# Reloads by full rows, strided weight-gradient stores and paced V loads in a memory-bound attention-block backward kernel

## Chip, cores, metric

One core of one Trainium2 chip. The metric is the device time of one launch in microseconds (us), and shorter is better. Executions of one kernel mostly agree within 0.3% to 0.4%. So differences of a few microseconds are read from repeated rounds on one chip, where each kernel runs in turn with the kernel before. A ratio is the mean time of one kernel's runs over that of the other's runs in the same rounds, so it is not quite the ratio of the medians that are quoted.

## The reference

Forward and backward of a decode block: an adaptive layer norm, cached attention over 32 heads and 8192 keys for a batch of 2, a gated feed-forward, and the gradients of everything, the caches included. Cut to what matters:

```python
x:(2,1,512)  k_cache, v_cache:(2,32,8192,128)  wq:(512,4096)  wo:(4096,512)
w1,w3:(512,1376)  w2:(1376,512)  w_mod:(512,3072)          # all bfloat16
mod = silu(c) @ w_mod ;  h = LN(x)*(1+ca)+sa
q = h @ wq ; p = softmax(q·K/sqrt(128)) ; o = p·V ;  x = x + ga * (o @ wo)
x = x + gb * (silu(h2@w1) * (h2@w3)) @ w2
return out, d_x, d_k_cache, d_v_cache, d_wq, d_wo, d_w1, d_w3, d_w2, d_c, d_w_mod
```

K and V are 134 MB each. V is read nearly twice (once forward, once for its transposed product with the output's gradient), K once, and dK and dV are written once, 268 MB. That is almost all of the 713.56 MB that move.

## The kernel before

Work is laid out in slots. One slot is one group of eight 128x128 transposes on TensorE, and a head is eight slots. An "A" job does the forward of one head and a "C" job its backward. Between them, once per batch element, stands a "chain": output projection, feed-forward, their gradients. `t1` is the slot at which the second chain is done; behind it come some 31 C heads, and with them 196 small tasks that make the weight gradients. All big data lives in 21 buffers of 1 MB ("halves": half of one head's K or V, or of its dK or dV). SyncE's queue issues the loads in program order, and each waits until its buffer is free.

```python
def load_v(key, i, hf):
    t = htile()                                     # one of the 21 halves
    qd.dma_start(t[:], src_of(A_v_cache, i)[:, hf*HK:(hf+1)*HK, :])   # qd = nc.sync
    free["half"] -= 1
    V[(key, hf)] = t

def pump():                                         # called whenever a half is given back
    while loads and free["half"] - keep[0] >= 1:    # loads: sorted by the slot that needs them
        loads.pop(0)[2]()

def outer(store, dst, n, which, w2, q):             # dV or dK of head n, a quarter at a time
    ...
    nc.vector.tensor_tensor(pair(t[:, o:o+QK, :]), ..., ALU.mult)     # VectorE, 1.2 us
    if o + QK == HK:
        sq_.dma_start(src_of(dst, n)[:, hf*HK:(hf+1)*HK, :], t[:])    # sq_ = nc.gpsimd
        ...                                         # the half is given back six slots later

# weight gradients: a matmul of two rows, ScalarE's copy to a staging tile, a store from GpSimd's queue
for h0 in range(0, H, 4):
    def dst(st, h0=h0):
        sq_.dma_start(out_5.rearrange("(h p) d -> p h d", p=P)[:, h0:h0+4, :],
                      st[:, 0:4*D].rearrange("p (h d) -> p h d", h=4))
    wgrad(dst, [("O", (h0+k)*P, P, "d_attn", 0, D, k*D) for k in range(4)], 4)

def again(w, n):                                    # wq, w_mod a second time, in pieces of 1024 columns
    for pc in range(n-1, -1, -1):
        loads.insert(0, (0, 0, lambda pc=pc: load_piece(wqr, w, pc)))
    pump()

def chain_done():                                   # at slot t1
    wn.clear(); wo_v.clear(); release(4 + H // WH)
    for k in range(2):
        rowst[k] = hflat(); free["half"] -= 1
    pump()

per = max(1, -(-nt // max(1, room)))                # here 1: one task per slot from t1 on
for k, f in enumerate(tasks):
    at(t1 + 1 + k // per, PL_TASK, f)
```

## Time and profile before

| | |
|---|---|
| median of 6 runs (range) | 1751.83 us (1750.34 to 1755.11) |
| span of the profiled run | 1749.5 us |
| moved | 713.56 MB, 408 GB/s |
| busiest compute engine | TensorE, 79% |

The first lines are of the page of the kernel before: TensorE's granted clock, the mean busy share of the 16 DMA engines and what they moved, in 40 equal slices of the span, then the DMA queues (packets, MB, share of the engines' time). Queue 1 is the loads, queue 0 the stores, queues 8 and 14 fetch instructions.

```profile
PEclk9999999988978888888897888676755565765786
DMA  9999999999999999999999999999999999999997
GB/s 381 417 418 418 418 417 390 418 376 416 420 423 409 410 415 422 412 415 420 415 411 408 411 413 394 370 413 412 425 422 418 407 413 404 420 425 417 410 390 305
...
q1 hardware_dynamic: 73376, 425.81, 60.1%
q0 software_dynamic: 41216, 284.22, 39.1%
q8 instruction: 188, 3.08, 0.7%
```

The DMA engines are full in 39 of 40 slices: this is a kernel bound by its transfers. The next table is the view by windows. Its last three columns are TensorE's granted clock, the mean DMA share and GB/s.

```profile
core 0: us, PE busy (x) PEld busy (x) DVE busy (x) ACT busy (x) POOL busy (x), PEclk, DMA share, GB/s
1150.00:1200.00 50.00, 42.10 (x590) 40.28 (x588) 35.48 (x82) 30.36 (x38) 5.87 (x11) 0.59 1.01 413
1200.00:1225.00 25.00, 21.02 (x346) 19.94 (x343) 19.16 (x42) 14.03 (x17) 3.20 (x6) 0.63 1.01 420
1225.00:1300.00 75.00, 54.51 (x674) 41.39 (x673) 45.30 (x47) 47.55 (x78) 11.35 (x20) 0.64 1.01 424
1300.00:1650.00 350.00, 259.03 (x3194) 198.20 (x3192) 219.34 (x241) 216.20 (x329) 63.15 (x115) 0.60 1.01 416
1650.00:1735.00 85.00, 46.83 (x848) 44.15 (x848) 76.48 (x80) 41.26 (x57) 15.97 (x30) 0.74 0.96 391
1735.00:1749.00 14.00, 0.00 (x0) 0.00 (x0) 0.00 (x0) 0.00 (x0) 0.00 (x0) 0.50 0.29 120
```

In these windows everything is at 413 to 424 GB/s and a share of 1.01 until 1650 us. (Packets overlap a little: at the end of the trace packets of 309 ns follow each other every 306 ns on one engine, so a full engine shows just over 1.) Then it falls to 391 and 0.96, with VectorE busy 76.48 of 85 us. The view of the V loads' line gives, after the colon, the shortest, median and longest issue in ns, then the first and last start:

```profile
L177 SPq DMA_DIRECT2D half<-in_A_v_cache_dram x252: 327/328/6146, 22.4 to 1648.6; - x126
```

So behind 1648.6 us only stores are issued, and nearly all that moves in the last 85 us is stores. The view of the load queue's own waits for 1190 to 1225 us:

```profile
SPq L177 <- DMA out_dram<-half: 20.6, 4, 8.9
SPq L177 <- PE tp L366: 6.9, 2, 5.1
```

Here the loads wait for their buffers (for a store that has to land, or for the transposes that still read the buffer), at most 8.9 us at a time.

### The profile page before, as it was taken

What the parts mean: (1) busy time and instruction counts of PE and PEld (TensorE: products, weight loads), DVE (VectorE), ACT (ScalarE), POOL (GpSimd) and SP (SyncE); (2) the same over time, 40 slices, a digit from 0 to 9 for tenths busy, and PEclk for the clock granted to TensorE, in tenths of its full rate; (3) what the DMA queues carried; (4) which work ended last, traced back from release to release, by engine and by line L of the source; (5) the groups of instructions that cost most, each with busy time, mean ns of one, the idle gap of its engine ahead of it and who ended that gap; (6) DMA issues with size and microseconds to landing.
All of it is one profiled execution on the core that took longest, in us unless ns stands there. A gap on an engine that the chain in (4) does not pass through costs nothing. (4 is left out here: it accounts for less than half of the span.)

```text
span 1749.5 us, 54974 instructions
## 1 busy us (share of the span) xinstructions
PE 1374.4 (79%) x24112; PEld 1227.8 (70%) x24112; DVE 1170.0 (67%) x1677; ACT 980.9 (56%) x1404; POOL 393.6 (22%) x685
## 2 busy tenths in 40 slices
PE   6999999989977767777777778788686877767662
PEld 5999998979866767676676668778554655655562
DVE  2666666857776676667667668777566675756596
ACT  4666666646544445455454555565655675765562
POOL 0334333312221222122122222111112121112121
PEclk9999999988978888888897888676755565765786
DMA  9999999999999999999999999999999999999997
GB/s 381 417 418 418 418 417 390 418 376 416 420 423 409 410 415 422 412 415 420 415 411 408 411 413 394 370 413 412 425 422 418 407 413 404 420 425 417 410 390 305
DMA packets 114845, 713.56 MB, mean 408 GB/s; under 512 B 11392, under 2 KB 20300, under 8 KB 33196
## 3 DMA queue, kind: packets, MB, share of 16 engines
q1 hardware_dynamic: 73376, 425.81, 60.1%
q0 software_dynamic: 41216, 284.22, 39.1%
q8 instruction: 188, 3.08, 0.7%
q14 instruction: 53, 0.43, 0.1%
q10 hardware_dynamic: 12, 0.01, 0.0%
HBM read 425.79 MB, written 284.20 MB: 406 GB/s over the span
## 5 line engine op out<-in xcount | busy, mean ns | idle before, releaser
L371 ACT COPY kt<-tp 128x1024 bf16<-128x1024 bf16 x768 | 774.9, 1015 | 532.8 <-PE tp L366 524.4
L366 PE MATMUL tp<-identb,half 128*128 128x128 bf16 x8192 | 767.7, 249 | 2.8 <-DMA half<-in_A_k_cache_dram 1.4
L366 PEld LDWEIGHTS <-half 128*128 128x128 bf16 x8192 | 596.6, 112 | 116.7 <-issue 111.7
L1093 POOL DMA_DIRECT2D out_dram<-half x256 | 136.7, 534 | 966.8 <-DVE half L1088 810.1
L427 PE MATMUL m_ps<-ek,half 128*128 128x129 bf16 x4096 | 327.0, 222 | 0.2
L369 DVE COPY kt<-tp 128x1024 bf16<-128x1024 bf16 x256 | 175.8, 687 | 188.7 <-PE tp L366 183.6
L1065 PE MATMUL s_ps<-DO_bf,kt 128*128 128x1 bf16 x4096 | 191.3, 168 | 102.2 <-DVE kt L369 70.1
L1065 PEld LDWEIGHTS <-kt 128*128 128x128 bf16 x4096 | 186.4, 107 | 117.7 <-DVE kt L369 78.4
L386 PE MATMUL s_ps<-qT_bf,kt 128*128 128x1 bf16 x4096 | 177.8, 164 | 99.3 <-DVE kt L369 98.4
L427 PEld LDWEIGHTS <-half 128*128 128x128 bf16 x4096 | 247.7, 98 | 0.4 <-issue 0.2
L386 PEld LDWEIGHTS <-kt 128*128 128x128 bf16 x4096 | 159.6, 98 | 104.2 <-DVE kt L369 102.5
L1213 ACT CAST stg<-m_ps 128x512 bf16<-128x512 f32 (+2 forms) x123 | 72.0, 591 | 111.7 <-DMA out_dram<-stg 86.3
L1212 PE MATMUL m_ps<-half 2*128 2x512 bf16 (+2 forms) x123 | 72.3, 588 | 27.0 <-ACT stg L1213 25.2
L449 PE MATMUL k_ps<-half,pz 128*32 128x512 bf16 x1024 | 68.7, 389 | 21.0 <-POOL pz L435 21.0
L449 PEld LDWEIGHTS <-pz 128*32 128x32 bf16 x1024 | 21.8, 97 | 41.8 <-POOL pz L435 23.2
L1313 ACT COPY kt<-tp 128x1024 bf16<-128x1024 bf16 x28 | 28.6, 1048 | 6.7 <-PE tp L1306 6.6
L398 DVE TENSOR_REDUCE nm<-s_ps 128x1 f32<-128x128 f32 x64 | 18.4, 287 | 20.4 <-PE s_ps L395 20.4
L395 PE MATMUL s_ps<-nident,rm 128*128 128x128 bf16 x64 | 15.2, 238 | 20.6 <-DVE rm L390 20.6
L1190 ACT CAST half<-m_ps 2x512 bf16<-2x512 f32 (+1 forms) x36 | 19.9, 564 | 16.5 <-DMA out_dram<-half 7.8
L712 PE MATMUL tp<-identb,half 128*128 128x128 bf16 x256 | 28.0, 277 | 0.0
L1306 PE MATMUL tp<-identb,half 128*128 128x128 bf16 x224 | 20.1, 242 | 9.0 <-DMA half<-in_A_wq_dram 4.7
L712 PEld LDWEIGHTS <-half 128*128 128x128 bf16 x256 | 23.8, 135 | 0.0
(878 smaller groups left out, 1784.2 us busy)
## 6 DMA issues: line engine op xcount, KB each, us to landing
out_dram<-half POOLq DMA_DIRECT2D x256, 1024.0 KB, 12.4
half<-in_A_v_cache_dram SPq DMA_DIRECT2D x252, 1024.0 KB, 12.9
half<-in_A_k_cache_dram SPq DMA_DIRECT2D x128, 1024.0 KB, 19.8
out_dram<-stg POOLq DMA_DIRECT2D x22, 512.0 KB, 17.0
half<-in_A_wq_dram SPq DMA_DIRECT2D x8, 1024.0 KB, 14.9
half<-in_w_mod_dram SPq DMA_DIRECT2D x6, 1024.0 KB, 16.0
half<-in_B_w_dram SPq DMA_DIRECT2D x6, 1024.0 KB, 15.2
half<-in_A_wo_dram SPq DMA_DIRECT2D x4, 1024.0 KB, 20.5
```

Source lines behind the costliest of these rows:

```text
L366: nc.tensor.transpose(tp[:, j, :], block(j), identb[:])
L369: nc.vector.tensor_copy(kt[:], tp[:])
L371: nc.scalar.copy(kt[:], tp[:])
L386: nc.tensor.matmul(S_ps[i][:, cc:cc + 1], kt[:, j, :], qT_bf[:, h, b:b + 1], start=True, stop=True)
L427: nc.tensor.matmul(m[:, 0:P + 1], vb_(i, kk), t[:, kk % QK, 0:P + 1], start=(kk == 0), stop=(kk == KK - 1), skip_group_check=True)
L449: nc.tensor.matmul(kp["ps"][NR * j:NR * (j + 1), :], pz[:, o:o + NR], K[(i, kk // HK)][:, kk % HK:kk % HK + QP, :], start=False, stop=(h = ...
L712: nc.tensor.transpose(tp[:, n * NC + dc, :], wo_of(h, dc), identb[:])
L1065: nc.tensor.matmul(DP[n][:, cc:cc + 1], kt[:, j, :], DO_bf[:, b, h:h + 1], start=True, stop=True)
L1093: sq_.dma_start(src_of(dst, n)[:, hf * HK:(hf + 1) * HK, :], t[:])
L1212: nc.tensor.matmul(ps[:lw, 0:rw], rsl(ln, lc, lw), rsl(rn, rc, rw), start=True, stop=True)
L1213: nc.scalar.copy(st["t"][:lw, o:o + rw], ps[:lw, 0:rw])
L1313: nc.scalar.copy(kt[:], tp[:])
```

## The change

Its intent: larger packets for the weight matrices that are read again and for dwo and dw2, gradient stores on ScalarE's queue, gradient tasks spread over the whole stretch, and, behind the second chain, V loads that come in bursts and no longer run as far ahead as the buffers allow, so that reads are left to mix with the stores at the end. The core of the diff, with cuts:

```diff
     def pump():
         while loads and free["half"] - keep[0] >= 1:
-            loads.pop(0)[2]()
+            need = loads[0][0]
+            if not pace["lot"]:
+                loads.pop(0)[2]()
+                continue
+            n = min(pace["lot"], len(loads))
+            if need > now[0] + pace["lead"]() or (free["half"] - keep[0] < n and need > now[0] + HG):
+                return
+            for k in range(min(n, free["half"] - keep[0])):
+                issued[0] = None
+                loads.pop(0)[2]()
+                if k == 0 and issued[0] is not None:
+                    tc.add_manual_dep(issued[0].ins, turned_last[0].ins.name, ...,
+                                      reason="loads keep pace with the heads")
 ...
-            nc.tensor.transpose(tp[:, j, :], block(j), identb[:])
+            turned_last[0] = nc.tensor.transpose(tp[:, j, :], block(j), identb[:])
 ...
+    def by_rows(outp, ln, rn, n):          # dwo, dw2: every fourth row per matmul, RT = 4
+        for r0 in range(0, n, RT * P):
+            ...
+                gq.dma_start(outp[r0:r0 + RT * np_].rearrange("(p r) d -> p (r d)", r=RT), st[:np_, 0:RT * D])
+            wgrad(dst, [(ln, r0 + k, np_, rn, 0, D, k * D) for k in range(RT)], RT)
 ...                                        # all gradient stores: gq = nc.scalar in place of nc.gpsimd
+            qd.dma_start(rows[kc], src[kc * P:(kc + 1) * P, :])     # wq, w_mod again, by full rows
 ...
     def chain_done():
         ...
+        pace["lot"] = 4
+        pace["lead"] = lambda: max(NG + NG // 2, 6 * NG - (now[0] - t1) // 2)
         pump()
 ...
-    per = max(1, -(-nt // max(1, room)))
+    def slot_of(k):
+        return t1 + 1 + k * room // nt
     for k, f in enumerate(tasks):
-        at(t1 + 1 + k // per, PL_TASK, f)
+        at(slot_of(k), PL_TASK, f)
+    for k, f in again:
+        want(slot_of(k) - NG, f)
```

`lot` is how many loads go out together, and `lead` how many slots ahead of its use a load may be placed: here 48 at `t1`, shrinking to 12 (`NG` is 8, the slots of a head). `add_manual_dep`: the first V load of each lot waits, on the chip, for the transposes that stand last in the program at the point where the lot is placed.

More of the change, by code (lines that the diff above doesn't have):

```diff
@@ L163 @@
     V = {}
+    issued = [None]
+    turned_last = [None]
     def src_of(ap, i):
@@ L176, in load_v @@
         t = htile()
-        qd.dma_start(t[:], src_of(A_v_cache, i)[:, hf * HK:(hf + 1) * HK, :])
+        issued[0] = qd.dma_start(t[:], src_of(A_v_cache, i)[:, hf * HK:(hf + 1) * HK, :])
         free["half"] -= 1
@@ L327, in want @@
         loads.append((need, seq[0], f))
+    pace = {"lot": 0, "lead": lambda: 0}
     def pump():
         while loads and free["half"] - keep[0] >= 1:
-            loads.pop(0)[2]()
+            need = loads[0][0]
[9 more added lines that the diff above has]
+                if k == 0 and issued[0] is not None:
+                    tc.add_manual_dep(issued[0].ins, turned_last[0].ins.name,
+                                      mybir.DependencyInfo(mybir.DependencyClass.Sync, mybir.DependencyReason.DATA),
+                                      reason="loads keep pace with the heads")
     def release(n=1):
@@ L1198, in row_of, with rsl, wgrad @@
             later(lambda c0=c0: part(c0))
-    def rsl(name, c0, w):
+    def rsl(name, c0, w, step=1):
         k, pb, o = rmap[name]
-        return rowst[k][pb:pb + B, o + c0:o + c0 + w]
-    def wgrad(dst, pieces, n):
+        return rowst[k][pb:pb + B, o + c0:o + c0 + (w - 1) * step + 1:step]
+    gq = nc.scalar
+    RT = 4
+    def wgrad(dst, pieces, step=1):
         st = {}
@@ L1211, in one @@
             ps = mtps()
-            nc.tensor.matmul(ps[:lw, 0:rw], rsl(ln, lc, lw), rsl(rn, rc, rw), start=True, stop=True)
+            nc.tensor.matmul(ps[:lw, 0:rw], rsl(ln, lc, lw, step), rsl(rn, rc, rw), start=True, stop=True)
             nc.scalar.copy(st["t"][:lw, o:o + rw], ps[:lw, 0:rw])
@@ L1226, with dst @@
     row_of("d_ffn", d_ffn_bf, NC, 96)
-    for h0 in range(0, H, 4):
-        def dst(st, h0=h0):
-            sq_.dma_start(out_5.rearrange("(h p) d -> p h d", p=P)[:, h0:h0 + 4, :],
-                          st[:, 0:4 * D].rearrange("p (h d) -> p h d", h=4))
-        wgrad(dst, [("O", (h0 + k) * P, P, "d_attn", 0, D, k * D) for k in range(4)], 4)
+    def by_rows(outp, ln, rn, n):
+        for r0 in range(0, n, RT * P):
+            np_ = min(RT * P, n - r0) // RT
+            assert (n - r0) % RT == 0
+            def dst(st, r0=r0, np_=np_):
+                gq.dma_start(outp[r0:r0 + RT * np_].rearrange("(p r) d -> p (r d)", r=RT), st[:np_, 0:RT * D])
+            wgrad(dst, [(ln, r0 + k, np_, rn, 0, D, k * D) for k in range(RT)], RT)
+    by_rows(out_5, "O", "d_attn", HD)
     for outp, nm in ((out_6, "d_gate"), (out_7, "d_up")):
@@ L1235, in dst @@
             def dst(st, kc=kc, outp=outp):
-                sq_.dma_start(outp[kc * P:(kc + 1) * P, :], st[:, 0:F])
-            wgrad(dst, [("h2", kc * P, P, nm, c0, min(512, F - c0), c0) for c0 in range(0, F, 512)], 3)
-    for f0 in range(0, FC, 4):
-        nf = min(4, FC - f0)
-        def dst(st, f0=f0, nf=nf):
-            full = [f for f in range(f0, f0 + nf) if fsz(f) == P]
-            if full:
-                sq_.dma_start(out_8[f0 * P:(f0 + len(full)) * P].rearrange("(k p) d -> p k d", p=P),
-                              st[:, 0:len(full) * D].rearrange("p (k d) -> p k d", d=D))
-            if len(full) < nf:
-                k = nf - 1
-                sq_.dma_start(out_8[(f0 + k) * P:F, :], st[:FL, k * D:(k + 1) * D])
-        wgrad(dst, [("hh", (f0 + k) * P, fsz(f0 + k), "d_ffn", 0, D, k * D) for k in range(nf)], nf)
+                gq.dma_start(outp[kc * P:(kc + 1) * P, :], st[:, 0:F])
+            wgrad(dst, [("h2", kc * P, P, nm, c0, min(512, F - c0), c0) for c0 in range(0, F, 512)])
+    by_rows(out_8, "hh", "d_ffn", F)
     x2 = col("x2")
@@ L1261, in out_row @@
         nc.scalar.copy(r[:], tp[:B, 0:NC, :].rearrange("p k d -> p (k d)"))
-        sq_.dma_start(dst, r[:])
+        gq.dma_start(dst, r[:])
     def task_x2():
@@ L1273, with turned, load, tr @@
     later(task_x2)
-    wqr = {}
-    def again(w, n):
-        for pc in range(n - 1, -1, -1):
-            loads.insert(0, (0, 0, lambda pc=pc: load_piece(wqr, w, pc)))
-        pump()
-    def before_last(n, f):
-        tasks.insert(len(tasks) - n, f)
+    again = []
+    acc = {}
+    def turned(src, n, vec, name):
+        rows = {}
+        hold = {}
+        steps = [(kc, m0) for kc in range(NC) for m0 in range(0, n, GRP)]
+        assert n % GRP == 0
+        def load(kc):
+            rows[kc] = hflat()[:, 0:n * P]
+            free["half"] -= 1
+            qd.dma_start(rows[kc], src[kc * P:(kc + 1) * P, :])
+        def tr(k):
+            kc, m0 = steps[k]
+            if k == 0:
+                acc[name] = mtps()
+            tp = tps.tile([P, GRP, P], BF16, name="tp", tag="tp")
+            for j in range(GRP):
+                nc.tensor.transpose(tp[:, j, :], rows[kc][:, (m0 + j) * P:(m0 + j + 1) * P], identb[:])
+            if m0 + GRP == n:
+                rows.pop(kc)
+                release()
+                pump()
+            kt = ktp.tile([P, GRP, P], BF16, name="kt", tag="kt")
+            nc.scalar.copy(kt[:], tp[:])
+            hold[k] = kt
+        def mm(k):
+            kc, m0 = steps[k]
+            kt = hold.pop(k)
+            a = acc[name][:, 0:NC * B].rearrange("p (k b) -> p k b", b=B)
+            for j in range(GRP):
+                nc.tensor.matmul(a[:, kc, :], kt[:, j, :], vec[:, m0 + j, :],
+                                 start=(k == 0 and j == 0), stop=(m0 + j == n - 1),
+                                 skip_group_check=True)
+        for k in range(len(steps) + 1):
+            if k < len(steps) and steps[k][1] == 0:
+                again.append((len(tasks), lambda kc=steps[k][0]: load(kc)))
+            later(lambda k=k: (tr(k) if k < len(steps) else None, mm(k - 1) if k else None))
     row_of("dq", hv(DQ_bf), H, 32)
@@ L1291, in dst @@
             def dst(st, kc=kc, half=half, w=w):
-                sq_.dma_start(out_4[kc * P:(kc + 1) * P, half * w:(half + 1) * w], st[:, 0:w])
-            wgrad(dst, [("h1", kc * P, P, "dq", half * w + c0, 512, c0) for c0 in range(0, w, 512)], 4)
-    acc = {}
-    def turned(n, vec, name):
-        hold = {}
-        def tr(m0):
-            if m0 == 0:
-                acc[name] = mtps()
-            tp = tps.tile([P, GRP, P], BF16, name="tp", tag="tp")
-            for k in range(2):
-                for kc in range(NC):
-                    nc.tensor.transpose(tp[:, k * NC + kc, :],
-                                        piece(wqr, kc, m0 + k), identb[:])
-            if (m0 + 2) * P % PW == 0:
-                wqr.pop(m0 * P // PW)
-                release()
-                pump()
-            kt = ktp.tile([P, GRP, P], BF16, name="kt", tag="kt")
-            nc.scalar.copy(kt[:], tp[:])
-            hold[m0] = kt
-        def mm(m0):
-            kt = hold.pop(m0)
-            a = acc[name][:, 0:NC * B].rearrange("p (k b) -> p k b", b=B)
-            for k in range(2):
-                for kc in range(NC):
-                    nc.tensor.matmul(a[:, kc, :], kt[:, k * NC + kc, :], vec[:, m0 + k, :],
-                                     start=(m0 == 0 and k == 0 and kc == 0), stop=(m0 + k == n - 1),
-                                     skip_group_check=True)
-        later(lambda: tr(0))
-        for m0 in range(2, n, 2):
-            later(lambda m0=m0: (tr(m0), mm(m0 - 2)))
-        later(lambda: mm(n - 2))
+                gq.dma_start(out_4[kc * P:(kc + 1) * P, half * w:(half + 1) * w], st[:, 0:w])
+            wgrad(dst, [("h1", kc * P, P, "dq", half * w + c0, 512, c0) for c0 in range(0, w, 512)])
     d_h1 = col("d_h1")
@@ L1345, in task_dx0 @@
         out_row(d_x0, out_1.rearrange("b s d -> (b s) d"))
-    before_last(12, lambda: again(wq_d, HD // PW))
-    turned(H, hv(DQ_bf), "h1")
+    turned(A_wq, H, hv(DQ_bf), "h1")
     later(task_dh1)
@@ L1357, in dst @@
             def dst(st, kc=kc, m0=m0, w=w):
-                sq_.dma_start(out_10[kc * P:(kc + 1) * P, m0:m0 + w], st[:, 0:w])
-            wgrad(dst, [("sc", kc * P, P, "d_mod", m0 + c0, 512, c0) for c0 in range(0, w, 512)], 4)
-    before_last(12, lambda: again(wm_d, MD // PW))
-    turned(MC, d_mod_bf, "c")
+                gq.dma_start(out_10[kc * P:(kc + 1) * P, m0:m0 + w], st[:, 0:w])
+            wgrad(dst, [("sc", kc * P, P, "d_mod", m0 + c0, 512, c0) for c0 in range(0, w, 512)])
+    turned(w_mod, MC, d_mod_bf, "c")
     def task_dc():
@@ L1382 @@
     room = max(sC) - NG - t1 - 2
-    per = max(1, -(-nt // max(1, room)))
+    assert room > 0
+    def slot_of(k):
+        return t1 + 1 + k * room // nt
     for k, f in enumerate(tasks):
-        at(t1 + 1 + k // per, PL_TASK, f)
+        at(slot_of(k), PL_TASK, f)
+    for k, f in again:
+        want(slot_of(k) - NG, f)
+    loads.sort(key=lambda x: x[:2])
     pump()
```

## The prediction

> **What bounds the kernel.** The DMA engines: in the page's slices their share is nine tenths or more in 39 of 40, 408 GB/s over the span; no compute engine passes 79%. 713.56 MB at the achieved rate is the time, so only a better rate or fuller engines shorten it. All of the change lies behind the second chain, whose first task (the dq matmuls, by the view of that line) runs at 1221 us. About 525 us and 217 MB are in play there, at a mean of 413 GB/s.
>
> In the table of windows, 1225 to 1650 us runs at 417 GB/s with a DMA share of 1.01, but 1650 to 1735 us at 391 GB/s and 0.96: the last V load is issued at 1648.6 us, after that there are only stores, and VectorE, which makes the dV and dK tiles, is busy 76.5 of 85 us. The loads had run ahead as far as buffers allowed, so the end has no reads to mix in and is bound by VectorE, about 10.6 us per head instead of about 15 us by DMA.
>
> **What the change does, costed with the trace's packet records.**
> 1. wq and w_mod by full rows: 3584 packets of 2 KB at 85.3 ns, against 77 ns per 2 KB of an 8 KB packet (309 ns). Saving 3584 x 8 ns / 16 engines = 1.8 us. The Trainium skill, "DMA: Bandwidth & Descriptors", section "Why small descriptors are slow (HBM only)", gives a fixed cost per packet; the trace agrees in direction.
> 2. Strided dwo and dw2: their stores are already recorded as 4 KB packets (164.5 ns; other 4 KB stores 159). At most 0.4 us.
> 3. Gradient stores from ACT's queue instead of POOL's. Same page, "Issuing engines are not separate DMA queues": all share the 16 engines, so no bandwidth. It frees about 25 us of waiting in POOL's queue, off the critical path.
> 4. Tasks spread over the whole room: gradient stores and w_mod loads move toward the end. With lead shrinking to 12 slots reads are held back, stores get buffers (VectorE waits 84 us for them in 1150 to 1650 us), and the last lot is issued about 20 slots before the last head. The write-only tail should shrink from 85 us to 25 to 40 us: 50 us x (418 - 391)/418 = 3 to 4 us.
> 5. Against it, lots alternate mixed and write-only stretches. Windows with half reads ran at 420 to 426 GB/s, with a quarter reads 405 to 415, write-only near 407 per full share. Two thirds at 421 and one third at 407 is 416, today's rate. Lots themselves: 0 to 4 us.
>
> Sum: 1.8 + 3.5 + 2 + small, about 8 us. Ceiling: all 217 MB at 424 GB/s would save 14 us; 2% (35 us) is out of reach.
>
> **Prediction:** 1743.5 us, range 1735 to 1750. Faster by over 2%: 0.03, within 2%: 0.95, slower: 0.02.
>
> **What the profile would show.** No 2 KB read packets after 1221 us; last V load 40 to 60 us nearer to the end; DMA share 1.0 until the last 30 us, VectorE no longer full for 85 us; 417 to 422 GB/s behind 1221 us; less waiting of VectorE for store buffers; gradient stores on a third queue; nothing changed before 1221 us.
>
> **What would make it wrong.** Loads held too short: PE waits for V and the DMA share dips between lots (slower). Long write-only stretches under 405 GB/s that eat the tail's gain. Or bursts of reads raise the mixed rate above 424 GB/s, unseen in this trace (below 1735 us).

## The result

| | before | changed |
|---|---|---|
| median us (range, runs) | 1752.03 (1750.04 to 1756.29, 20) | 1750.92 (1747.54 to 1754.23, 10) |
| ratio, 95% interval | | 0.9991 (0.9982 to 1.0001) |

The outputs are correct. The time is the same within 2%, as forecast, but only 1.1 us went away where 8 had been forecast, and the measured time is outside the stated range of 1735 to 1750. The same lines of the page of the changed kernel, now with a queue 10, which is ScalarE's with the gradient stores:

```profile
PEclk9999999988988978887888888665855565586585
DMA  9999999999999999999999999998999999999997
GB/s 380 417 417 417 418 417 389 417 378 416 419 423 407 413 418 422 412 409 421 412 413 407 421 407 390 379 407 336 419 422 422 415 412 419 419 418 418 425 418 295
...
q1 hardware_dynamic: 70832, 425.81, 59.7%
q0 software_dynamic: 36864, 268.45, 36.9%
q10 hardware_dynamic: 5019, 15.78, 2.3%
```

And its windows:

```profile
core 0: us, PE busy (x) PEld busy (x) DVE busy (x) ACT busy (x) POOL busy (x), PEclk, DMA share, GB/s
1150.00:1200.00 50.00, 43.45 (x564) 41.63 (x561) 34.50 (x79) 29.81 (x38) 5.87 (x11) 0.51 1.01 412
1200.00:1225.00 25.00, 22.11 (x353) 21.08 (x352) 18.71 (x41) 13.84 (x17) 3.20 (x6) 0.57 0.73 286
1225.00:1300.00 75.00, 56.36 (x768) 45.01 (x766) 56.82 (x59) 51.82 (x82) 11.19 (x21) 0.68 1.01 420
1300.00:1650.00 350.00, 262.76 (x3168) 204.62 (x3165) 222.86 (x247) 217.07 (x331) 43.15 (x81) 0.57 1.01 418
1650.00:1735.00 85.00, 44.31 (x790) 41.23 (x790) 61.09 (x64) 40.99 (x54) 12.78 (x24) 0.66 1.01 421
1735.00:1749.00 14.00, 0.00 (x0) 0.00 (x0) 0.00 (x0) 0.00 (x0) 0.00 (x0) 0.50 0.29 123
```

Two windows differ most. The end did what was predicted: 421 GB/s in place of 391 over 1650 to 1735 us, the engines full. But 1200 to 1225 us fell from 420 to 286 GB/s with a share of 0.73, which as an estimate from the two windows costs 25 x (420 - 286) / 420 = 8 us. The V loads' line and the load queue's waits for 1190 to 1225 us say what is missing there:

```profile
L179 SPq DMA_DIRECT2D half<-in_A_v_cache_dram x252: 327/328/5981, 22.5 to 1682.0; - x126
```

```profile
SPq L179 <- PE tp L383: 25.9, 1, 25.9
SPq L179 <- DMA out_dram<-half: 7.7, 1, 7.7
```

One single wait of 25.9 us for transposes. In the trace no load is issued between 1194.6 and 1221.0 us; in the kernel before eight were issued between 1200 and 1219 us. So there are two questions. Does that wait cost what the end has gained? And did the full end bring what its windows promise?

### The profile page after: what moved, and what is told of

The parts are those of the page before. It is cut to its first block, busy times and chain, and to the rows that moved or that the text cites. A ratio compares the mean times of both kernels' runs of the same rounds, so it can differ in the third digit from the quotient of the medians.

```text
span 1752.4 us, 54847 instructions
## 1 busy us (share of the span) xinstructions
PE 1382.9 (79%) x24113; PEld 1242.4 (71%) x24113; DVE 1168.4 (67%) x1677; ACT 985.1 (56%) x1405; POOL 370.5 (21%) x646
## 3 DMA queue, kind: packets, MB, share of 16 engines
q0 software_dynamic: 36864, 268.45, 36.9%
## 5 line engine op out<-in xcount | busy, mean ns | idle before, releaser
L388 ACT COPY kt<-tp 128x1024 bf16<-128x1024 bf16 x768 | 773.8, 1014 | 585.1 <-PE tp L383 573.9
L383 PE MATMUL tp<-identb,half 128*128 128x128 bf16 x8192 | 779.6, 252 | 3.9 <-DMA half<-in_A_k_cache_dram 1.5
L383 PEld LDWEIGHTS <-half 128*128 128x128 bf16 x8192 | 606.6, 113 | 91.4 <-issue 85.3
L1082 PEld LDWEIGHTS <-kt 128*128 128x128 bf16 x4096 | 191.9, 109 | 135.6 <-DVE kt L386 110.3
L444 PEld LDWEIGHTS <-half 128*128 128x128 bf16 x4096 | 246.6, 98 | 0.2
L403 PEld LDWEIGHTS <-kt 128*128 128x128 bf16 x4096 | 159.2, 98 | 107.6 <-DVE kt L386 105.7
L1315 ACT COPY kt<-tp 128x1024 bf16<-128x1024 bf16 x28 | 28.6, 1044 | 9.3 <-PE tp L1309 9.2
L729 PE MATMUL tp<-identb,half 128*128 128x128 bf16 x256 | 30.0, 292 | 0.0
L1309 PE MATMUL tp<-identb,half 128*128 128x128 bf16 x224 | 20.4, 245 | 8.5 <-DVE kt L386 8.2
L729 PEld LDWEIGHTS <-half 128*128 128x128 bf16 x256 | 25.8, 143 | 0.0
L735 ACT COPY kt<-tp 128x1024 bf16<-128x1024 bf16 x16 | 16.2, 1012 | 14.2 <-PE tp L729 13.6
## 6 DMA issues: line engine op xcount, KB each, us to landing
out_dram<-half POOLq DMA_DIRECT2D x256, 1024.0 KB, 14.6
```

Of the source, the lines that this page charges most:

```text
L383: turned_last[0] = nc.tensor.transpose(tp[:, j, :], block(j), identb[:])
L388: nc.scalar.copy(kt[:], tp[:])
L403: nc.tensor.matmul(S_ps[i][:, cc:cc + 1], kt[:, j, :], qT_bf[:, h, b:b + 1], start=True, stop=True)
L444: nc.tensor.matmul(m[:, 0:P + 1], vb_(i, kk), t[:, kk % QK, 0:P + 1], start=(kk == 0), stop=(kk == KK - 1), skip_group_check=True)
L729: nc.tensor.transpose(tp[:, n * NC + dc, :], wo_of(h, dc), identb[:])
L1082: nc.tensor.matmul(DP[n][:, cc:cc + 1], kt[:, j, :], DO_bf[:, b, h:h + 1], start=True, stop=True)
```

## The experiments

The theories, as named in the expectations: **A**, the gain at the end is real and is paid back at the one wait ahead of 1221 us. **B**, a kernel with full engines can't gain by moving reads about, and the hole is only where the moved reads are missing. Later came **C**: the end waits for one DMA engine that is behind the other fifteen, so that the mean share misleads.

### 1. The first wait taken out (e1_first_free)

```diff
-                if k == 0 and issued[0] is not None:
+                if k == 0 and issued[0] is not None and now[0] > t1:
```

A dependency is taken away here that protects no data; buffers are still waited for.

> Theory A (the tail's gain was real and was paid back at one place: the first paced load waits for the transposes of the second chain's last slot, so the load queue issues nothing from 1195 to 1221 us and the DMA share falls to 0.5 to 0.7 in 1205 to 1225 us): with only that first wait taken out the hole is gone, 1200 to 1250 us is back above 415 GB/s, the tail stays full, and the time is 1742 to 1744 us, ratio to before about 0.995. Theory B (a kernel whose engines are full cannot gain by moving reads; the hole is only where the moved reads are missing, and filling it empties the end again): 1749 to 1752 us, with the tail below 400 GB/s again or another dip.

Measured: 1745.99 us median against 1751.83 of before in the same rounds, ratio 0.9969 (0.9957 to 0.9982). 1200 to 1250 us ran at 422 GB/s. The hole is gone and the time falls by 5.8 us. That is for A, though 2 us less than A had said. The end stays full, as A said: the 85 us from 1640 to 1725 us ran at 421 GB/s and a share of 1.01. (The window of the tables above, 1650 to 1735 us, shows 384 here, because this kernel is nearly through by then: its span is 1742.4 us.)

### 2. The rows without the pace (e2_rows_only)

```diff
-        pace["lot"] = 4
-        pace["lead"] = lambda: max(NG + NG // 2, 6 * NG - (now[0] - t1) // 2)
```

> The change without the lots and the lead (by rows, strided, other queue, tasks spread). Theory A: no hole at 1200 us, packets of wq and w_mod save about 2 us, spread gradient stores help the end by 1 us or so: 1748 to 1750 us, tail of stores only still there. Theory B: 1749 to 1752 us. This run tells how much of the gain belongs to the rows.

Measured: 1749.12 us, ratio 0.9986 (0.9973 to 0.9998), some 2.5 us. No hole (421 GB/s in 1200 to 1225 us), and 395 GB/s at the end. That is about what the prediction gave to the packets and the stores, but it isn't shown that they earned it: experiment 14 finds 2.7 us behind the last packet that the new stores and their queue save, as much as the whole gain here. The run of experiment 1, in the same rounds, differs from this one by the pace (without its first wait) and is 3.1 us faster by the medians (1745.99, intervals overlapping).

### 3. The pace alone on the kernel before (e5_pace_only)

The edit is the `pump`, `pace` and `turned_last` part of the diff above, put into the kernel before.

> The lots and the lead alone on the kernel before. Theory A: the same hole at 1195 to 1221 us (about 9 us), a tail filled for the most part (4 us), no packet gain: 1754 to 1758 us. Theory B: 1750 to 1753 us.

Measured: 1754.11 us, ratio 1.001 (0.9998 to 1.0023). The time is as A said, but not the place: 1200 to 1225 us had no hole (420 GB/s). The load queue did stop, but only from 1194.1 to 1208.6 us. The reason lies on TensorE: its granted clock in that stretch was 0.76 to 1.0 in this execution, against 0.50 to 0.57 in the changed kernel's, and the program up to there is the same. The wait ends when TensorE arrives at `t1`, so how long the hole lasts depends on TensorE's clock, in a kernel that otherwise isn't bound by TensorE. All sixteen traces agree: the first task behind `t1` begins at 1208.0 and 1209.5 us in the two with a clock of 0.86 and 0.90 in 1200 to 1225 us, and at 1213.3 to 1223.9 us in the others (0.57 to 0.81). This run lost its time elsewhere: 1600 to 1650 us at 360 GB/s, where the load queue waited 38.1 us for transposes in one piece. Why the old reload code makes that wait so long was not followed up.

### 4. No wait of any lot (e3_no_gate)

```diff
-                if k == 0 and issued[0] is not None:
+                if False:
```

> Lots and lead in program order only, no load ever waits for a transpose. Theory A: no hole; loads go out when their buffer is free, so they run ahead again and the tail is partly as before: 1746 to 1750 us. Theory B: 1749 to 1752 us. If it is as good as the run with only the first wait out, the waits of the later lots are worth nothing.

Measured: 1748.94 us, ratio 0.9981 (0.9967 to 0.9994). Better than the changed kernel, as A says; 3 us behind the first experiment by the medians, with overlapping intervals, so whether the waits of the later lots are worth anything stays open.

### 5 and 6. The changed kernel and the one without its first wait, side by side (e6_after_again, e7_first_free_again)

The edits: none, and that of experiment 1.

> The changed kernel once more, unaltered, so that it stands beside the others on one chip. Theory A: ratio to before 0.997 to 1.001; the load queue again issues nothing between about 1195 us and the dq matmuls, and how long that is goes with the granted clock of TensorE in 1150 to 1225 us (0.5: 26 us without a load; 0.9 to 1.0: about 14).

> The same as the first experiment, beside the changed kernel. Theory A: 3 to 8 us faster than the changed kernel in the same rounds, ratio to before 0.996 to 0.998. Theory B, with the first result laid to the chip: within 2 us of it.

Measured on one chip in the same rounds (the trace of e6 has the hole again, 305 GB/s in 1200 to 1225 us): changed kernel 1752.47 us, ratio 1.0009 (0.9997 to 1.0021); without the first wait 1746.28 us, ratio 0.9973 (0.9961 to 0.9985). The ranges of the runs don't touch (1750.82 to 1753.78, 1745.48 to 1746.64). The wait costs 6.2 us. Windows and load queue of the version without it:

```profile
core 0: us, PE busy (x) PEld busy (x) DVE busy (x) ACT busy (x) POOL busy (x), PEclk, DMA share, GB/s
1150.00:1200.00 50.00, 42.72 (x587) 40.86 (x585) 35.46 (x81) 29.64 (x38) 6.24 (x12) 0.57 1.01 417
1200.00:1225.00 25.00, 22.85 (x348) 21.61 (x349) 18.97 (x39) 14.38 (x19) 3.36 (x7) 0.57 1.01 421
1225.00:1300.00 75.00, 56.29 (x759) 44.56 (x757) 55.79 (x58) 51.39 (x82) 10.66 (x20) 0.66 1.01 422
1300.00:1650.00 350.00, 261.88 (x3150) 205.00 (x3148) 222.51 (x246) 216.01 (x329) 43.69 (x82) 0.56 1.01 418
1650.00:1735.00 85.00, 44.16 (x790) 40.88 (x790) 59.77 (x63) 40.40 (x53) 12.26 (x23) 0.66 0.94 390
1735.00:1749.00 14.00, 0.00 (x0) 0.00 (x0) 0.00 (x0) 0.00 (x0) 0.00 (x0) 0.58 0.03 13
```

```profile
SPq L179 <- DMA out_dram<-half: 20.8, 3, 8.2
SPq L179 <- PE tp L383: 14.1, 3, 7.3
```

1200 to 1225 us is full again and each of the queue's waits is 8.2 us at most, as in the kernel before (8.9). The kernel also ends sooner, which is why its last two windows look emptier (over 1640 to 1725 us it moves 417 GB/s at a share of 1.01). A is shown as far as the hole goes, and B is refuted there: the filled hole is worth 6.2 us and the end stays full. It is also the version that beats both kernels.

### 7. The first wait eight slots later (e8_late8)

```diff
-        pace["lead"] = lambda: max(NG + NG // 2, 6 * NG - (now[0] - t1) // 2)
+        pace["lead"] = lambda: -99 if now[0] < t1 + 8 else max(NG + NG // 2, 6 * NG - (now[0] - t1) // 2)
         pump()
+        at(t1 + 8, PL_TASK, pump)
```

> The suspected cost made larger: the first paced loads wait for the transposes of a slot eight later than now. Theory A: the stretch without loads grows by eight slots, 10 to 14 us, and with the stores at half to two thirds of the rate there the kernel is 4 to 8 us slower than the changed one: 1755 to 1759 us. Theory B: not over 2 us slower, since reads not made there are made later beside the same stores.

Measured: 1754.36 us, ratio 1.0013 (0.9996 to 1.0031), so 1.9 us over the changed kernel by the medians, with overlapping intervals. The stretch without loads did grow, from 24.9 us (e6, 1192.95 to 1217.9) to 36.9 us (1196.2 to 1233.1), but it cost less than the 4 us that A had asked for. By the time alone that is what B forecast (not over 2 us), so A's rule that a longer hole costs in proportion failed here; the six runs spread widely (1748.19 to 1756.71). The stores' timeline of this run suggests why a later hole is cheap (start, length, engine, line, what it waited for):

```profile
1202.70 0.53 POOL L1110 DMA_DIRECT2D out_dram<-half  x1 [3.29 <-DVE prod L748]
1207.61 0.53 POOL L1110 DMA_DIRECT2D out_dram<-half  x1 [4.37 <-DVE SIG L754]
1211.30 0.53 POOL L1110 DMA_DIRECT2D out_dram<-half  x1 [3.15 <-DVE ds L1126]
1216.45 0.53 POOL L1110 DMA_DIRECT2D out_dram<-half  x1 [4.62 <-DVE half L1105]
1220.28 0.53 POOL L1110 DMA_DIRECT2D out_dram<-half  x1 [3.29 <-DVE prod L748]
...
1230.92 0.53 POOL L1110 DMA_DIRECT2D out_dram<-half  x1 [3.26 <-DVE half L1105]
1233.29 0.53 POOL L1110 DMA_DIRECT2D out_dram<-half  x1 [1.83 <-DVE half L1105]
1236.69 0.53 POOL L1110 DMA_DIRECT2D out_dram<-half  x1 [2.87 <-DVE half L1105]
1238.43 0.53 POOL L1110 DMA_DIRECT2D out_dram<-half  x1 [1.20 <-DVE ds L1126]
```

While the chain's last steps run, a 1 MB store comes every 4.4 us on average (1202.70 to 1220.28), about 240 GB/s, and the loads have to fill the rest. From 1230.92 us on they come every 2.5 us, over 400 GB/s, nearly enough to fill the engines without any load. The trace of e7 bears it out: no load is issued there between 1248.7 and 1303.1 us, and yet 1250 to 1303 us ran at 421 GB/s and a share of 1.01. In these traces a hole in the loads costs only while the stores are thin.

### 8. The lead held at 48 slots (e9_lead48)

```diff
 (edit of experiment 1, and)
-        pace["lead"] = lambda: max(NG + NG // 2, 6 * NG - (now[0] - t1) // 2)
+        pace["lead"] = lambda: 6 * NG
```

> The first wait taken out and the lead held at 48 slots instead of shrinking to 12. If the shrinking lead is what fills the end (the term of 3 to 4 us in the prediction): the last V load is 20 us or more earlier, the stretch of stores alone and below 400 GB/s is back, and the time is 2 to 4 us over the run with the first wait out alone. If the end is filled by something else (the spread tasks): within 1 us of it.

Measured, in the rounds of 5 and 6: 1747.86 us, ratio 0.9981 (0.9968 to 0.9994), 1.6 us over the run with the first wait out alone. Its last V load is at 1659.9 us, 14.7 us earlier than there. Both are less than the expectation asked for (2 to 4 us, 20 us or more). By the time alone the shrinking lead is worth 1 or 2 us, with overlapping intervals. By the bytes it should be worth far more. This is worked out from the packet records of the four traces, one execution each, as the time between two amounts of data moved since the start (the last packet without instruction fetches):

```
                     480 to 500 MB   500 to 710 MB   710 MB to last packet   last packet at
before                   48.4 us         508.5 us           13.2 us            1743.8 us
changed                  56.9            500.5              18.5               1749.4
first wait out (e7)      48.1            501.7              20.0               1741.9
and lead 48 (e9)         47.5            508.5              14.2               1743.0
```

The first column is the hole: 8.5 us. The second is what the prediction counted on: the shrinking lead brings 710 MB 7 to 8 us sooner. The third column takes most of that back: the last 3 MB need 18 to 20 us in place of 13 to 14. The other traces of these two kernels, e6 and e1, give the same: 500.0 and 500.9 us, then 18.8 and 19.7. In these four traces the end is a ramp: engines finish one after another over some 14 us, and for the last 5 to 10 us a single one of the sixteen is at work. That is where theory C came from. (From the last packet to the end of the span it is 5.8 us in the kernel before and 3.0 to 3.1 us in the other three: see experiment 14.)

Each store increments its semaphore once per engine, so the first and last of the 16 increments show the fastest and the slowest engine. For two stretches of stores, from the trace's semaphore increments:

```
kernel before, its last stores            first of 16    second last     last of 16
  store issued at 1698 us (1697.8)          1701.82                       1708.80
  store issued at 1733.5 us (the last)      1738.87        1740.13        1744.23
  mean time between the LAST increments of successive stores, 1671 to 1723 us: 2.64 us (longest 2.79)
first wait out (e7)
  its last store, issued at 1723.3 us       1727.93        1732.36        1742.25
  mean time between the LAST increments, 1700 to 1745 us: 2.49 us (longest 2.66)
```

A store is eight 8 KB packets per engine, one every 306 ns when nothing else runs, 2.45 us. In the kernel before the slowest engine completed a store every 2.64 us, and it never ran out of stores: at each of these increments the next store had been issued at least 8 us before. That is the very stretch where the mean share said that 4% of the engines' time was idle. As far as that idle time was lack of work, it belonged to the others. (Why the late engine needed 2.64 us and not 2.45 is open.)

### 9 to 12. Extra work for 16, 8, 7 and 4 engines at the end (e15_extra16, e14_extra8, e16_extra7, e17_extra4)

The kernel before, with useless loads behind its last V load (N = 16, 8, 7, 4):

```diff
     assert not loads
+    xt = [ekp.tile([P, 2048], BF16, name="extra", tag="ek") for _ in range(3)]
+    for k in range(36):
+        qd.dma_start(xt[k % 3][0:N, :], A_wq[N * (k % 8):N * (k % 8) + N, 0:2048])
```

The Trainium skill, "DMA: Bandwidth & Descriptors", section "Why a DMA increments its semaphore by 16 and not by 1", says that such a DMA uses as many engines as divide its rows, up to 16, and on this kind of queue the lowest-numbered ones. The traces agree on the number: one of these loads brought late increments from 16, 8, 7 and 4 engines. Which engines they are no trace shows; that rests on the page. Each engine that takes part gets 36 packets of 159 ns, 5.7 us of work.

> The kernel before with 36 useless loads of 8 rows by 4 KB after its last V load, so each lands on 8 of the 16 DMA engines and gives each of those 36 packets of about 159 ns, 5.7 us of work, in the stretch of stores alone. Theory C (the end waits for one DMA engine that is behind the others, and idle time of the other fifteen in that stretch is not to be had): either 0 to 1 us slower, when the late engine is not among the eight, or 5 to 6 us slower, when it is. Mean-share theory (the step of the prediction that reckoned with 4% idle engines, 3.4 us over 85 us): the 2.9 us per engine on average vanish in that idle time, 0 to 1 us slower.

> The same with 16 rows, so that all 16 engines get 5.7 us of extra work in the stretch of stores alone. Theory C: the late engine was never idle there, so all of it shows: 5 to 6.5 us slower than before, 1756.5 to 1758. Mean-share theory: 3.4 us of it vanish in the idle time of that stretch, about 2 us slower.

> The extra loads with 7 rows instead of 8, so that by the Trainium skill they fall on the seven lowest DMA engines and leave the eighth alone. If the delay of the 8-row run came from one late engine and that is the eighth (number 7): 0 to 1.5 us slower than before. If the late engine is one of the first seven, or if any extra loads at the end delay it whatever engine they use: 5 to 6.5 us slower again.

> The same with 4 rows, on the four lowest engines. Late engine number 7, or 4 to 6: 0 to 1 us slower than before. Any extra loads delay the end: 5 us or more. The mean share of the sixteen would allow 1.4 us of extra work per engine on average.

| rows | median us | before, same rounds | ratio (95%) | in us |
|---|---|---|---|---|
| 16 | 1756.34 | 1750.34 | 1.0039 (1.0024 to 1.0053) | +6.8 |
| 8 | 1756.84 | 1750.34 | 1.0035 (1.0023 to 1.0048) | +6.1 |
| 7 | 1757.12 | 1753.07 | 1.0031 (1.0015 to 1.0048) | +5.4 |
| 4 | 1752.17 | 1753.07 | 0.9996 (0.9982 to 1.001) | -0.7 |

(The last column is the ratio less one, times the median of before.) The line of the extra loads in the run with 8 rows, and of the one with 4, shows that they were issued in the same stretch in both:

```profile
L1397 SPq DMA_DIRECT2D extra<-in_A_wq_dram x36: 272/272/1152, 1648.1 to 1727.9; - x36
```

```profile
L1397 SPq DMA_DIRECT2D extra<-in_A_wq_dram x36: 247/250/1162, 1650.4 to 1726.5; - x36
```

Sixteen engines or seven, about the whole 5.7 us show (4.1 to 6.5 us by the medians), and no run with 7 or more rows was as fast as the median of its kernel before; four, and nothing shows. Nothing of it vanished in the 3.4 us of idle time that the mean share promised. So it isn't extra loads as such that delay the end: it is extra work for one engine, which by the page's numbering is one of the fifth to seventh. It must be the late one itself, if the last store is as in the trace of the kernel before: an engine that is 4.1 us ahead of it (1740.13 against 1744.23) would with 5.7 us more work end only 1.6 us later. In the run with 8 rows the first of the 16 increments of the last store came at 1738.86 us, as in the kernel before (1738.87), while the last came at 1749.43 in place of 1744.23. C is shown. My guess in the expectations that it would be number 7 was wrong.

### 13. Lots of one (e10_lot1)

```diff
 (edit of experiment 1, and)
-        pace["lot"] = 4
+        pace["lot"] = 1
```

> First wait taken out, lots of one in place of lots of four, the lead unchanged. The prediction gave the lots themselves 0 to 4 us. If bursts of reads help: 2 us or more slower than lots of four (over 1748). If lots are worth nothing: 1745 to 1747 us, ratio to before 0.996 to 0.998.

Measured: 1746.53 us, ratio 0.9977 (0.9966 to 0.9989), the same as with lots of four. Bursts as such are worth nothing that these rounds can see.

### 14. The gradient stores on GpSimd's queue (e12_pool)

```diff
 (edit of experiment 1, and)
-    gq = nc.scalar
+    gq = nc.gpsimd
```

> First wait taken out, the gradient stores back on GpSimd's queue. As predicted for step 3 the queue is worth no bandwidth: within 1.5 us of the run with the first wait out alone, 1745 to 1748 us. A rival: the third queue is what took part of the gain (or gave it), then over 2 us apart.

Measured, in the rounds of 13: 1747.13 us, ratio 0.9985 (0.9972 to 0.9997), 0.6 us over lots of one by the medians and 1.4 us by the ratios, intervals overlapping. Within what was expected: no bandwidth from another queue, as the Trainium skill, "DMA: Bandwidth & Descriptors", section "Issuing engines are not separate DMA queues", has it.

But the traces show that the queue counts behind the last packet. The kernel ends with a barrier of all engines, and GpSimd reaches it only when its closing `DRAIN` is over. Here is GpSimd's `DRAIN` in the view of the program's last line, in the kernel before and then in e7 (count; shortest, median and longest in ns; first and last start; the longest is the one that starts first):

```profile
L1417 POOLq DRAIN  x3: 40/102/15260, 1733.5 to 1749.3; - x3
```

```profile
L1436 POOLq DRAIN  x3: 40/93/20839, 1723.3 to 1744.6; - x3
```

So the long one ends at 1748.8 us in the kernel before, 4.5 us after the last increment of the last store (1744.23), and at 1744.1 us in e7, 1.8 us after it (1742.25). From the last increment to the end of the span it is 5.3 us in all six traces with the old stores on GpSimd's queue (before, e5, e14 to e17), 4.1 us in this run's, and 2.6 us in all nine with the new stores on ScalarE's queue. That is 2.7 us for the change: 1.5 us by the queue and 1.2 us by the rest (the row forms and their places in the program). Why the drain lasts so long is not shown.

## Why the prediction was wrong

- **What bounds the kernel:** right. The time went with the transfers in all runs, but for what stands behind the last packet (experiment 14).
- **Step 1, packets by full rows (1.8 us), and step 2, strided stores (at most 0.4 us):** seen, but the gain is not shown. The changed trace has no 2 KB read packets behind 1221 us, where the kernel before has 3584. The run without the pace gained about 2.5 us, but 2.7 us lie behind the last packet (experiment 14), so that the sum fits is luck.
- **Step 3, the other queue:** no bandwidth, which is not contradicted (0.9985 against 0.9977). "Off the critical path" was wrong at the very end: GpSimd's closing drain is 1.5 us shorter with the stores on the other queue (experiment 14).
- **"Nothing changed before 1221 us":** wrong, and this is the first step that failed. The prediction read `t1` as a time and took the new wait for a brake that acts behind it. But the load queue runs ahead of TensorE: in the kernel before, eight loads were issued between 1200 and 1219 us, ahead of the first task behind `t1` at 1221 us, as their buffers came free. The new wait holds the first of them until TensorE arrives at `t1`, just where the stores are thin. The queue stood still for 26.4 us, 1200 to 1225 us fell from 420 to 286 GB/s, and without that wait the kernel is 6.2 us faster (experiments 5 and 6). The prediction's list of dangers had named a dip "between lots", not ahead of the first.
- **Step 4, the tail (3 to 4 us), and the lots (2 us):** the mechanism came as described. The last V load moved from 1648.6 to 1682.0 us (33 us, forecast 40 to 60), and 1650 to 1735 us is full at 421 GB/s. But the step from the mean share to time failed, and this is the second step that failed. In place of 3.5 + 2 us, the shrinking lead measured 1.6 us of time (medians, 1.4 us by the ratios; experiment 8) and the lots nothing (experiment 13); the whole pace without its first wait measured 3.1 us (experiments 1 and 2). The last engine never ran out of work at the end, and work added to it showed in full (experiments 8 to 12), so filling the others brought 710 MB sooner and the last packet hardly.
- **"Bound by VectorE at the end":** wrong for the same reason. VectorE paced the engines that were ahead; the last one was behind them, with stores waiting.
- **"Less waiting of VectorE for store buffers":** wrong in sign. In 1225 to 1650 us that wait rose from 83.8 to 119.3 us. A half comes free only when all sixteen increments of its store are in, and the median time of a dK or dV store from issue to landing rose from 12.4 to 14.6 us; that this is the reason is not shown.

The balance, from same-round medians: without the first wait the change is worth 4.5 to 5.8 us in place of 8, and 2.7 us of that is the shorter drain behind the last packet, which the prediction did not have. What it did have brought an estimated 1.8 to 3.1 us (the difference). The first wait takes 6.2 us back; 1.1 us was left in the first rounds and none in the second.

Open: why one engine is late, which of three it is, and how its lag builds up; why GpSimd's closing drain lasts as long as it does; whether the larger packets save anything; and what the waits of the later lots are worth. The trace of experiment 14 took 506.1 us from 500 to 710 MB, where e1 and e7 took 501 to 502, in an execution 3 us over its median; that was not followed up.

## What to carry to other kernels

A wait that ties a load to a place in the program also holds the loads that the queue would have issued ahead of it: look at what the queue does before that place, start such pacing where the stores alone fill the engines, and mind that an engine whose clock varies moves the end of the wait. When transfers are the bound, a mean share over sixteen engines can hide the last one: look at the first and the last semaphore increment of a store before idle percents are turned into microseconds. Compare also what stands between the last packet and the end. To find out whether idle time can be had, add useless work there and see if the time grows.

## What the Trainium skill lacked or had wrong

- "DMA: Bandwidth & Descriptors", section "Latency and other measured facts", says that engines 7 and 15 are usually the slower ones. Here extra work on the four lowest engines cost nothing (0.9996) and on the seven lowest 5.4 us (1.0031), so with the page's own numbering the late engine was one of numbers 4 to 6.
- The same page doesn't say how far the engines drift apart under a steady queue of stores, or that a mean share hides it (in its part on the iDMA fabric it says, in passing, that a bulk load runs at the pace of its slowest engine): at the end the last engine was 4.1 us behind the second last in the kernel before, and 5.0 to 9.9 us in the four traces of the changed kernel and of the one without its first wait.
- The same page, section "Why small descriptors are slow (HBM only)", gives about 3 cycles per packet. The median times here, 84, 159 and 309 ns for 2, 4 and 8 KB, and 9 ns for the 4 bytes of a semaphore increment, fit a constant 9 ns per packet, of which successive packets of one engine overlap 3 ns; by the page's 850 MHz, 3 cycles would be an estimated 3.5 ns. (Whether the page's cycles and these records measure the same thing no run shows.)
- No page says how long GpSimd's closing drain lasts, or what it goes by: here it ended 4.5 us after the last store had landed with the gradient stores of the kernel before on GpSimd's queue, and 1.8 us after it with the new ones on ScalarE's.
